# Expert tiles given out unit by unit and run beside the recurrence's chunks, every engine in written order

## The chip, the cores and the metric

The kernel runs on one core of one Trainium2 chip. The metric is the device time of one execution in microseconds (us). Before the change it is 980.18 us, the median of three runs (979.2 to 986.29).

The engines are PE (matrix multiply; PEld is its weight load), DVE (vector), ACT (scalar and activation), POOL (GpSimd) and SP (which here only issues transfers). Sixteen DMA engines move data. ACT and POOL issue transfers too.

## The reference, cut to what matters

```python
# recurrence: batch 4, heads 8, seq 768, head_dim 48, all float32
for t in range(S):
    state = alpha[:, :, t, :, None] * state + k[t] (outer) v[t]
    y[:, :, t] = q[t] @ state
x = y rearranged to (3072, 384)                 # rows = tokens
# router and experts: E = 8, F = 1024
noisy = x @ w_gate + log1p(exp(x @ w_noise)) * noise
top2, top2_w = the two largest of noisy per row, softmax over the two
out[row] = sum over its two experts e of  w * (relu(x[row] @ w1[e]) @ w2[e])
```

## The kernel before, in words

**Recurrence (`fast_gla`).** The 3072 tokens are 24 chunks of 128 (six chunks for each of four sequences). `prepare(n)` turns a, k and q of a chunk with PE transposes into the PSUM tile `tp` (L197). ACT copies a to `a_s` (L203), checks it with a Relu (L205) and copies k (L208). DVE runs the running product P as a scan (L211), multiplies q by it (L214) and takes its reciprocal (L216). POOL multiplies k by the reciprocal (L218). `scores(n)` makes the masked score matrix MT (PE L230, DVE L232) and `k_end` (L236, L238). `finish(n)` makes the state S (PE L247, DVE L253 or L256, POOL L257) and the output y (PE L260 from the old state, L265 from MT). `put_x` copies y out (L155), turns it for the router (L158, L159) and writes it to the DRAM tensor `x_rows` (L160, issued by SP).

**Router.** A unit is three chunks. After each unit, `router` makes the logits (L464), ACT takes exp and log (each with a table load, L468 and L484), DVE finds the top two and their weights, and PE counts ranks (L515, L516), so that every token knows its row in its expert's region of a DRAM `table`. POOL writes the entries with six indirect DMAs for a unit (L527). After the last unit `plan_tiles` computes from the counts which expert and which table row each of 55 tiles of 128 tokens has. `NTILE` = 55 covers the worst case of part-filled tiles.

**Experts.** For each tile, SP loads 128 table entries (L587) and the expert's w1 (L593, 1.5 MB, three buffers, two tiles ahead); POOL gathers the token rows (L596), reads the rows of a first expert from `half_rows` (L635), and writes either to `half_rows` (L641) or the sum to the output (L649). PE turns the rows (L603), does layer 1 (L616, 24 products of 128x128x128) and layer 2 (L623, 8 products with 384 columns); each float32 product shows as two instructions. All of w2 stays in SBUF.

**What sets the order.** A scheduler orders the instructions of each engine inside each of the two parts; the expert part begins after the recurrence part, because the plan needs all counts. `after(n)` puts the clearing of `table` (one transfer of 3200-byte rows, ACT), of `half_rows` (eight transfers of 1536-byte rows, SP) and the router's inputs at step 0, and the loading of w2 (eight transfers of 1.5 MB, SP) at step 2. Transfers issued by SP and ACT share eight semaphores: each new transfer waits until the last one on its semaphore has landed. POOL's transfers have eight others.

Of the kernel before, what the change touches and what calls it, by code (L numbers as in the profile page):

```python
# [18 lines left out]
def kernel(  # L19
# [23 lines left out]

    nc = tc.nc
# [17 lines left out]
    RMAX = N  # L62
    NTILE = (2 * N) // C + E - 1
    TROWS = E * RMAX + (E + 0) * C
    NONE = 2 * N
    RANGE = 1e-18

# [22 lines left out]
    expert_ids = const.tile([C, E], F32, name="expert_ids")  # L90
    region = const.tile([C, E], F32, name="region")
    for e in range(E):
        nc.gpsimd.memset(expert_ids[:, e:e + 1], float(e))
        nc.gpsimd.memset(region[:, e:e + 1], float(e * RMAX))
# [7 lines left out]
    tile_no = const.tile([1, NTILE], F32, name="tile_no")  # L102
    nc.gpsimd.iota(tile_no, pattern=[[1, NTILE]], base=0, channel_multiplier=0, allow_small_or_imprecise_dtypes=True)
    step_no = const.tile([1, RMAX // C], F32, name="step_no")
    nc.gpsimd.iota(step_no, pattern=[[C, RMAX // C]], base=0, channel_multiplier=0,
# [6 lines left out]
    nothing = const.tile([C, TROWS // C * 4], U32, name="nothing")  # L112
    nc.gpsimd.memset(nothing, NONE)
    zeros = const.tile([C, NT // 8, DM], F32, name="zeros")
    nc.gpsimd.memset(zeros, 0.0)

    def clear_table():
        nc.scalar.dma_start(out=table.rearrange("(p r) w -> p (r w)", p=C), in_=nothing)

    def clear_half():  # L120
        for i in range(8):
            nc.sync.dma_start(out=half_rows.rearrange("(i n p) d -> i p n d", i=8, p=C)[i], in_=zeros)

    NIN = 3
# [28 lines left out]
    def put_x(n, y, on, ps_tp, xT, at):  # L153
        y_sb = on.tile([C, DM], F32, name="y_sb")
        nc.scalar.copy(y_sb, y.rearrange("p h d -> p (h d)"))  # L155
        tp = ps_tp.tile([C, NP, C], F32, tag="tp", name="tp")
        for a in range(KO):
            nc.tensor.transpose(tp[:, a, :], y_sb[:, ds(a * C, C)], ident)  # L158
        nc.scalar.copy(xT[:, :, ds(at * C, C)], tp[:, 0:KO, :])  # L159
        nc.sync.dma_start(out=x_rows[ds(n * C, C), :], in_=y_sb)  # L160


    def fast_gla(es, after):
        gc = pool("gc", 1, es)
        vp = pool("vp", 4, es)
        kp = pool("kp", 2, es)
        sp = pool("sp", 2, es)
        xtp = pool("xtp", 2, es)
        rp = pool("rp", 2, es)
        ps_sc = pool("ps_sc", 1, es, space=PS)  # L170
        ps_tp = pool("ps_tp", 3, es, space=PS)
        ps_y = pool("ps_y", 3, es, space=PS)
        ins = {x: [gc.tile([C, H, DP], F32, name=f"{x}_in{i}") for i in range(NIN)] for x in "akq"}
# [4 lines left out]
        a_s = [gc.tile([C, NP, C + 1], F32, name=f"a_s{i}") for i in range(2)]  # L178
        P_s = [gc.tile([C, NP, C + 1], F32, name=f"P_s{i}") for i in range(3)]
        for t in a_s:  # L180
            nc.vector.memset(t[:, :, 0:1], 0.0)
        least = gc.tile([C, NP, C + 1], F32, name="least")
        nc.vector.memset(least, RANGE)
        nc.vector.memset(least[:, :, 0:1], 1.0)
        P_end = gc.tile([C, NT, NP], F32, name="P_end")
        above = gc.tile([C, NT], F32, name="above")
        less_1 = gc.tile([C, 1], F32, name="less_1")
        nc.vector.memset(less_1, -1.0)
        MTs = [gc.tile([C, 2, NP, C], F32, name=f"MT{i}") for i in range(2)]
# [3 lines left out]

        def transposed(src):
            tp = ps_tp.tile([C, NP, C], F32, tag="tp", name="tp")
            for j in range(NP):
                nc.tensor.transpose(tp[:, j, :], src[:, 2 * j:2 * j + 2, :], ident)  # L197
            return tp

        def prepare(n):  # L200
            c = chunks[n]
            a_t = transposed(ins["a"][n % NIN])
            nc.scalar.copy(a_s[n % 2][:, :, 1:C + 1], a_t)  # L203
            over_1 = kp.tile([C, NP, C], F32, name="over_1")
            nc.scalar.activation(over_1, a_t, AF.Relu, bias=less_1, accum_out=above[:, n:n + 1])  # L205
            k_t = transposed(ins["k"][n % NIN])
            k_raw = kp.tile([C, NP, C], F32, name="k_raw")
            nc.scalar.copy(k_raw, k_t)  # L208
            q_t = transposed(ins["q"][n % NIN])
            P = P_s[n % 3]  # L210
            nc.vector.tensor_tensor_scan(P.rearrange("p j t -> p (j t)"), a_s[n % 2].rearrange("p j t -> p (j t)"),  # L211
                                         least.rearrange("p j t -> p (j t)"), 0.0, op0=ALU.mult, op1=ALU.max)
            c["q"] = kp.tile([C, NP, C], F32, name="q_P")
            nc.vector.tensor_mul(c["q"], q_t, P[:, :, 1:C + 1])  # L214
            over = kp.tile([C, NP, C], F32, name="over")
            nc.vector.reciprocal(out=over, in_=P[:, :, 1:C + 1])  # L216
            c["k"] = kp.tile([C, NP, C], F32, name="k_P")
            nc.gpsimd.tensor_tensor(c["k"], k_raw, over, op=ALU.mult)  # L218
            nc.gpsimd.tensor_copy(out=P_end[:, n, :, None], in_=P[:, :, C:C + 1])
            c["end"] = kp.tile([C, NP, 2], F32, name="end")  # L220
# [3 lines left out]
        def scores(n):  # L224
            c = chunks[n]
            sc = [ps_sc.tile([C, NP, C], F32, tag=f"sc{i}", name=f"sc{i}") for i in range(2)]
# [6 lines left out]
            if n % NCH != NCH - 1:  # L233
                tp = ps_tp.tile([C, NP, C], F32, tag="tp", name="tp")
                for j in range(NP):
                    nc.tensor.transpose(tp[:, j, :], c["k"][:, j, :], ident)  # L236
                c["k_end"] = kp.tile([C, NP, C], F32, name="k_end")
                nc.scalar.copy(c["k_end"], tp)  # L238

        def finish(n, xT, at):  # L240
            c = chunks.pop(n)
            first, last = n % NCH == 0, n % NCH == NCH - 1
            y = ps_y.tile([C, H, D], F32, tag="y", name="y")
            if not last:
                s1 = ps_y.tile([C, NP, 2, D], F32, tag="y", name="s1")
                for j in range(NP):
                    nc.tensor.matmul(s1[:, j], c["k_end"][:, j, :], c["v"][:, 2 * j:2 * j + 2, :], start=True,  # L247
                                     stop=True)
                S_new = kp.tile([C, NP * 2, D], F32, name="S_new")
                end = c["end"].rearrange("p j i -> p (j i)")[:, :, None].to_broadcast([C, NP * 2, D])  # L250
                s1 = s1.rearrange("p j i d -> p (j i) d")
                if first:
                    nc.vector.tensor_mul(S_new, s1, end)  # L253
                else:
                    S_sum = kp.tile([C, NP * 2, D], F32, name="S_sum")
                    nc.vector.tensor_add(S_sum, chunks["S"], s1)  # L256
                    nc.gpsimd.tensor_tensor(S_new, S_sum, end, op=ALU.mult)  # L257
            if not first:
                for j in range(NP):
                    nc.tensor.matmul(y[:, 2 * j:2 * j + 2, :], c["q"][:, j, :], chunks["S"][:, 2 * j:2 * j + 2, :],  # L260
                                     start=j == 0, stop=False, skip_group_check=True)
# [5 lines left out]
            if not last:  # L267
                chunks["S"] = S_new
            put_x(n, y, sp, ps_tp, xT, at)

        def load(n):
            chunks[n] = {"v": load_chunk(n, ins, vp)}

        load(0)
        load(1)
        prepare(0)
        load(2)
        prepare(1)
        scores(0)
        for n in range(NT):  # L280
            if n + 3 < NT:
                load(n + 3)
# [439 lines left out]
```

## Time and profile before

| what | value |
|---|---|
| median of the runs | 980.18 us |
| the profiled execution's own time | 982.83 us |
| its span | 981.1 us |
| mean granted PE clock over the span | 0.866 |
| recurrence, router, plan: until the first expert transpose | 0 to 369.6 us |
| 55 tiles: first layer-1 product to the last copy of a tile's sum | 371.2 to 969.2 us |
| after that, last scatter and end | 969.2 to 981.1 us |

The profiled execution took 1.7 us more than its span and 2.65 us more than the median. In the views below each line of a timeline is: start us, duration us, engine, source line, operation, out<-in, shape, count. A line of the windows view is: stretch, length, then busy time of PE, PEld, DVE, ACT, POOL (instruction counts in brackets), the granted PE clock, the DMA engines' busy share, GB/s. A queue line of the DMA view is: queue, packets, MB, share of the time of 16 engines.

### The profile page before, as it was taken

What the parts mean: (1) busy time and instruction counts of PE and PEld (TensorE: products, weight loads), DVE (VectorE), ACT (ScalarE), POOL (GpSimd) and SP (SyncE); (2) the same over time, 40 slices, a digit from 0 to 9 for tenths busy, and PEclk for the clock granted to TensorE, in tenths of its full rate; (3) what the DMA queues carried; (4) which work ended last, traced back from release to release, by engine and by line L of the source; (5) the groups of instructions that cost most, each with busy time, mean ns of one, the idle gap of its engine ahead of it and who ended that gap; (6) DMA issues with size and microseconds to landing.
All of it is one profiled execution on the core that took longest, in us unless ns stands there. A gap on an engine that the chain in (4) does not pass through costs nothing.

```text
span 981.1 us, 14593 instructions
## 1 busy us (share of the span) xinstructions
PE 879.0 (90%) x5393; PEld 738.9 (75%) x5393; DVE 268.1 (27%) x544; ACT 200.4 (20%) x370; POOL 347.9 (35%) x412
## 2 busy tenths in 40 slices
PE   5987879898797609999999999999999999999995
PEld 4876778797697607788788878887887788778873
DVE  7844584755855200011010101010101010101010
ACT  2412241333332201111111111111111111111110
POOL 3213143242342223344334433443444343434322
PEclk9955595676875558999999999999999999999998
DMA  9999162343410027544554555556555655665420
GB/s 236 292 371 211 32 128 56 66 97 63 84 41 9 17 74 264 210 169 157 195 203 156 172 203 192 176 176 217 193 179 185 216 196 180 198 218 168 160 66 3
DMA packets 164463, 152.85 MB, mean 156 GB/s; under 512 B 121704, under 2 KB 137755, under 8 KB 164384
## 3 DMA queue, kind: packets, MB, share of 16 engines
q1 hardware_dynamic: 144736, 127.53, 42.0%
q0 software_dynamic: 15616, 23.76, 7.2%
q10 hardware_dynamic: 4032, 0.53, 0.3%
q8 instruction: 46, 0.75, 0.3%
q14 instruction: 33, 0.27, 0.1%
HBM read 139.83 MB, written 31.57 MB: 175 GB/s over the span
## 4 chain that ended last, share of the span: by engine, by line
issue 44%; PE 22%; POOL 18%; DMA 7%; DVE 4%; ACT 2%; POOLq 1%; ACTq 0%; DVEq 0%; SPq 0%
POOL prev L635 6%; DMA half_rows<-o,tab 5%; POOL x_in L596 5%; PE y L265 5%; PE sc L230 4%; POOL out_dram L649 3%; PE tp L197 3%; PE s L247 3%; PE y L260 2%; PE lg L464 2%; POOL half_rows L641 2%; DVE over L216 1%; PE tp L158 1%; POOL table L527 1%; PE tp L236 1%
## 5 line engine op out<-in xcount | busy, mean ns | idle before, releaser
L616 PEld LDWEIGHTS h_ps<-xt,w 128*128 128x128 f32 x2640 | 304.8, 193 | 15.4 <-DVE xt L605 1.1
L616 PE MATMUL h_ps<-xt,w 128*128 128x128 f32 x2640 | 305.2, 276 | 0.7 <-DVE xt L605 0.7
L623 PE MATMUL o_ps<-w,h 128*128 x880 | 292.9, 486 | 0.0
L623 PEld LDWEIGHTS o_ps<-w,h 128*128 128x128 f32 x880 | 162.9, 190 | 102.0
L641 POOL DMA_INDIRECT half_rows<-o,tab x55 | 66.5, 1210 | 269.6 <-ACT o L634 263.4
L618 ACT ACTIVATE h<-h_ps 128x512 f32<-128x512 f32 x110 | 65.7, 597 | 265.6 <-PE h_ps L616 265.6
L648 DVE TENSOR_TENSOR both<-o,prev 128x384 f32<-128x384 f32 x55 | 30.8, 559 | 294.1 <-ACT o L634 281.3
L605 DVE COPY xt<-x_ps 128x384 f32<-128x384 f32 x55 | 30.7, 559 | 268.9 <-PE x_ps L603 268.9
L634 ACT ACTIVATE o<-o_ps,tab 128x384 f32<-128x384 f32 x55 | 32.0, 581 | 268.8 <-PE o_ps L623 268.8
L527 POOL DMA_INDIRECT table<-entry,place_u x48 | 48.7, 1015 | 104.7 <-DMA table<-entry,place_u 61.8
L216 DVE RECIPROCAL over<-P_s 128x512 f32<-128x512 f32 x24 | 80.4, 3348 | 0.6
L596 POOL DMA_INDIRECT x_in<-x_rows,tab x55 | 56.0, 1018 | 50.9 <-PE x_ps L603 38.3
L230 PE MATMUL sc<-q_P,k_P 48*128 48x128 f32 x384 | 50.7, 379 | 23.7 <-DVE den L486 10.2
L635 POOL DMA_INDIRECT prev<-half_rows,tab x55 | 58.3, 1059 | 38.4 <-DMA half_rows<-o,tab 28.4
L230 PEld LDWEIGHTS sc<-q_P,k_P 48*128 48x128 f32 x384 | 40.6, 260 | 33.3 <-issue 11.5
L265 PE MATMUL y<-vt,MT 128*128 128x48 f32 x384 | 65.5, 340 | 0.0
L265 PEld LDWEIGHTS y<-vt,MT 128*128 128x128 f32 x384 | 64.9, 262 | 0.1
L649 POOL DMA_INDIRECT out_dram<-both,tab x55 | 55.5, 1010 | 18.1 <-issue 16.5
L218 POOL TENSOR_TENSOR k_P<-k_raw,over 128x512 f32<-128x512 f32 x24 | 31.2, 1302 | 61.6 <-DVE over L216 23.5
L603 PE MATMUL x_ps<-ident,x_in 128*128 128x128 f32 x165 | 27.4, 276 | 28.5 <-DMA x_in<-x_rows,tab 28.5
L211 DVE TENSOR_TENSOR_SCAN P_s<-a_s,least 128x516 f32<-128x516 f32 x24 | 32.0, 1334 | 52.8 <-ACT a_s L203 52.7
L603 PEld LDWEIGHTS x_ps<-ident,x_in 128*128 128x128 f32 x165 | 20.1, 143 | 28.6 <-DMA x_in<-x_rows,tab 28.6
(119 smaller groups left out, 627.6 us busy)
## 6 DMA issues: line engine op xcount, KB each, us to landing
w<-in_moe_w_dram SPq DMA_DIRECT2D x63, 1536.0 KB
a_in<-in_alpha_dram SPq DMA_DIRECT2D x24, 192.0 KB
k_in<-in_k_dram SPq DMA_DIRECT2D x24, 192.0 KB
q_in<-in_q_dram SPq DMA_DIRECT2D x24, 192.0 KB
vt<-in_v_dram SPq DMA_DIRECT2D x24, 192.0 KB
half_rows<-zeros SPq DMA_DIRECT2D x8, 576.0 KB
x_rows<-y_sb SPq DMA_DIRECT2D x24, 192.0 KB
tab<-table SPq DMA_DIRECT2D x55, 2.0 KB
```

Of the source, the lines that this page charges most:

```text
L216: nc.vector.reciprocal(out=over, in_=P[:, :, 1:C + 1])
L230: nc.tensor.matmul(sc[i][:, j, :], c["k"][r, j, :], c["q"][r, j, :], start=True, stop=True)
L265: nc.tensor.matmul(y[:, h, :], MTs[n % 2][:, i, j, :], c["v"][:, h, :], start=first and h == 0, stop=h == H - 1, skip_group_check=True)
L527: nc.gpsimd.indirect_dma_start(out=table, out_offset=bass.IndirectOffsetOnAxis(ap=place_u[:, i:i + 1], axis=0), in_=entry.bitcast(U32)[:, ...
L596: nc.gpsimd.indirect_dma_start(out=x_in[i % NB], out_offset=None, in_=x_rows, in_offset=bass.IndirectOffsetOnAxis(ap=tabs[i][:, 0:1], axis=0),
L603: nc.tensor.transpose(x_ps[:, a, :], x_in[i % NB][:, ds(a * C, C)], ident)
L616: nc.tensor.matmul(h_ps[:, fo, :], w1[:, a, ds((half * FO // 2 + fo) * C, C)], xt[:, a, :], start=a == 0, stop=a == KO - 1)
L618: nc.scalar.activation(h[:, ds(half * FO // 2, FO // 2), :], h_ps, AF.Relu)
L623: nc.tensor.matmul(o_ps, h[:, fo, :], w2[:, ds(e, 1), fo, :].rearrange("p o d -> p (o d)"), start=fo == 0, stop=fo == FO - 1)
L635: get = nc.gpsimd.indirect_dma_start(out=prev[i % 2], out_offset=None, in_=half_rows, in_offset=bass.IndirectOffsetOnAxis(ap=tab[:, 3:4], ...
L641: put = nc.gpsimd.indirect_dma_start(out=half_rows, out_offset=bass.IndirectOffsetOnAxis(ap=tab[:, 2:3], axis=0), in_=o, in_offset=None, b ...
L649: put = nc.gpsimd.indirect_dma_start(out=out, out_offset=bass.IndirectOffsetOnAxis(ap=tab[:, 3:4], axis=0), in_=both, in_offset=None, boun ...
```

## The change

1. **Tiles per unit.** `plan_tiles(u)` now runs after every unit, on all 128 partitions. It gives out as many tiles as must already be full: `GIVEN` = 0, 5, 11, 17, 23, 29, 35, and all 55 after the last unit. Only the last unit's plan holds part-filled tiles. A table entry now holds token, weight, the other expert and the rank there; whether a token's first half has been stored is worked out per tile from these (`gather_x`: five small DVE instructions).
2. **Interleaving.** One list of steps n. Step n holds `prepare(n+2)`, `state(n)`, `turn_y(n-1)`, `scores(n+1)`, `route(n-1)`, `output(n)`, `load(n+3)`, `give(n-1)`, and beside them, in turn, the four quarters of each tile of that step. Steps 0 to 7 have no tile, step 10 has one, the other steps from 8 to 25 have two each (35 in all), and the last step holds the other 20.
3. **Order.** `tc.manual_schedule()` keeps every engine's instructions as written.
4. **Buffers.** PSUM (eight banks): `tp` 3 to 2, the bank tag `y` (s1, y, logits, ranks, totals) 3 to 1, layer-2 sums 2 to 1. SBUF: chunk inputs 3 to 2, w1 3 to 2, P 3 to 1, `a_s` and others 2 to 1, `x_in` 4 to 3. The Relu check writes back to the PSUM tile that it reads.
5. **Clearing.** `table` is cleared from a 16-byte pattern repeated 25,600 times, `half_rows` from a 512-byte pattern repeated 9,216 times, both issued by ACT after `prepare(1)`. `x_rows` writes move from SP to ACT. w2 is loaded at step 1, before `load(4)`.
6. **Waits.** The scatters into the table no longer wait for one another, but for the clearing.

```diff
+    GIVEN = [max(0, (2 * UT * (u + 1) - E * (C - 1) + C - 1) // C) for u in range(NU - 1)] + [NTILE]
...
     def clear_table():
-        nc.scalar.dma_start(out=table.rearrange("(p r) w -> p (r w)", p=C), in_=nothing)
+        entries.clear()
+        cleared = nc.scalar.dma_start(out=table.bitcast(F32).rearrange("(p r) w -> p r w", p=C),
+                                      in_=nothing[:, None, :].to_broadcast([C, TROWS // C, 4]))
+        entries.append(cleared.ins)
+    def put_entries(place, entry):
...
+        for earlier in entries[1:] + taken:
+            tc.declare_no_dep(put.ins, earlier, reason="different rows of the table")
+        tc.add_manual_dep(put.ins, entries[0].name, AFTER, reason="the table is cleared first")
...
     def clear_half():
-        for i in range(8):
-            nc.sync.dma_start(out=half_rows.rearrange("(i n p) d -> i p n d", i=8, p=C)[i], in_=zeros)
-    NIN = 3
+        nc.scalar.dma_start(out=half_rows.rearrange("(p n) (a d) -> p (n a) d", p=C, d=C),
+                            in_=zeros[:, None, :].to_broadcast([C, NT * KO, C]))
+    NIN = 2
...
+    def tile_steps(i, do, units):
+        def first():
+            load_w1(i + 1)
+            if i + 2 < units[1]:
+                gather_x(i + 2, units[0])
+            layer1(i, 0)
+        def second():
+            layer1(i, 1)
+        def third():
+            if i + 1 < units[1]:
+                turn_x(i + 1)
+            get_half(i)
+            layer2(i, 0)
+        def fourth():
+            layer2(i, 1)
+            combine(i)
+    def pools(es, name):
+        on = {"one": pool(name + "one", 1, es), "two": pool(name + "two", 2, es), "three": pool(name + "three", 3, es),
+              "tab": pool(name + "tab", 6, es)}
+        for x, bufs in (("h", 2), ("o", 1), ("tp", 2), ("sc", 1), ("y", 1)):
+            on[x] = pool(name + "ps_" + x, bufs, es, space=PS)
...
+        with tc.manual_schedule():
+            load(0)
+            load(1)
+            prepare(0)
+            load(2)
+            prepare(1)
+            load_router()
+            clear_table()
+            clear_half()
+            scores(0)
+            for n, tiles in enumerate(beside):
+                work = [step for i in tiles for step in steps_of(i)]
+                chunk = [lambda: prepare(n + 2), lambda: state(n), lambda: turn_y(n - 1), lambda: scores(n + 1),
+                         lambda: route(n - 1), lambda: output(n), lambda: load(n + 3), lambda: give(n - 1)]
+                if n == 1:
+                    load_w2()
...
+                if nxt and nxt[0] in starts:
+                    lo, u = nxt[0], unit_of[nxt[0]]
+                    some = range(lo, min(lo + 4, GIVEN[u]))
+                    chunk.insert(1, lambda: [load_tab(i) for i in some])
+                    chunk.insert(4, lambda: (load_w1(lo), [gather_x(i, u + 1) for i in some[:2]]))
+                    chunk.append(lambda: turn_x(lo))
+                for j in range(max(len(work), len(chunk))):
+                    if j < len(work):
+                        work[j]()
+                    if j < len(chunk):
+                        chunk[j]()
```

Arithmetic is the same in both. `state` is the first half of the old `finish`, `output` the second, `turn_y` and the logits part of `route` are taken from `put_x` and `router` and now run for each chunk, `choose` and `enter` are the rest of `router`, and `give` is `enter` and `plan_tiles`.

## The prediction, blind

> **What bounds the kernel now.** I read the page's shares first, then its 40 slices, then windows by stage, then the timeline of each stage.
>
> ```profile
> PE 879.0 (90%) x5393; PEld 738.9 (75%) x5393; DVE 268.1 (27%) x544; ACT 200.4 (20%) x370; POOL 347.9 (35%) x412
> ...
> PEclk9955595676875558999999999999999999999998
> DMA  9999162343410027544554555556555655665420
> ```
>
> PE bounds the whole, at two speeds: until slice 15 the granted clock is mostly about half, after it full. The windows show where the time stands.
>
> ```profile
> 44.00:76.00 32.00, 26.10 (x127) 23.01 (x128) 15.41 (x44) 7.08 (x14) 7.89 (x10) 0.54 1.07 372
> 148.00:172.00 24.00, 23.08 (x110) 21.98 (x111) 9.92 (x20) 4.26 (x10) 8.49 (x11) 0.50 0.27 58
> 339.00:369.00 30.00, 1.77 (x8) 1.59 (x8) 5.19 (x23) 0.00 (x0) 8.74 (x9) 0.50 0.22 75
> 369.00:969.00 600.00, 598.71 (x3685) 481.59 (x3685) 60.94 (x109) 97.08 (x164) 231.60 (x216) 1.00 0.53 181
> ```
>
> Four things: early on the DMA engines are full (372 GB/s); chunks then run with PE nearly busy at clock 0.50; for 30 us before the tiles PE idles for ranks, plan and gathers; and the tiles are 600 us of PE without a gap. The timeline gives a tile and a chunk at full clock:
>
> ```profile
> 947.67 5.52 PE L616 MATMUL h_ps<-xt,w 128*128 128x128 f32 x48
> 953.03 0.49 PE L603 MATMUL x_ps<-ident,x_in 128*128 128x128 f32 x3
> 953.36 5.33 PE L623 MATMUL o_ps<-w,h 128*128 x16
> 958.52 5.52 PE L616 MATMUL h_ps<-xt,w 128*128 128x128 f32 x48
> ```
>
> ```profile
> 28.42 0.49 PE L158 MATMUL tp<-ident,y_sb 128*128 128x128 f32 x3
> 28.74 0.60 PE L197 MATMUL tp<-ident,a_in 128*128 128x128 f32 x4
> ...
> 34.64 1.10 PE L247 MATMUL s<-vt,k_end 128*128 128x96 f32 x8
> 35.58 0.49 PE L158 MATMUL tp<-ident,y_sb 128*128 128x128 f32 x3
> ```
>
> A tile is 958.52 - 947.67 = 10.85 us. A chunk is 35.58 - 28.42 = 7.16 us, plus 0.8 for its logits (L464, six passes): 7.95.
>
> **The change, in four stretches of time.**
>
> *Stretch A: to the end of step 7, no tile beside.* It has two terms.
>
> First, transfers. In the new order of SP, w2 stands before load(4), and in the order of semaphores its third transfer waits for the table's clearing and its fifth for the clearing of half_rows. So load(4), which step 2 needs first, comes behind all early traffic, and PE stands still after steps 0 and 1. I add that traffic at full engines. The first four chunk loads and noise end near 19 us, as they do now. w2: 8 x 1.57 MB at 372 GB/s, 33.8. The clearing of half_rows, 576 pieces of 512 bytes per engine: a 192-byte piece costs 15 ns (the loads ran at about 208 GB/s over 16 engines) and a 1536-byte one 66 ns (372 GB/s); on the line between them 27 ns, 15 us. The table, 1600 pieces of 16 bytes per engine, is not in the trace; its nearest rows are the 32-byte reads at the start (window 0 to 3 us) and the 64-byte packets of the table's scatters (343 to 360 us):
>
> ```profile
> q10 hardware_dynamic: 319, 0.01, 6.0%
> ```
>
> ```profile
> q0 software_dynamic: 192, 0.01, 1.2%
> ```
>
> 6.0% of 16 x 3 us over 319 packets is 9 ns; 1.2% of 16 x 17 us over 192 is 17 ns. So 14 to 27 us by these, up to 106 us if a piece cost what a 1536-byte one does. I take 10 ns, 16 us, as the 32-byte reads are nearest in size and use the same kind of queue. x_rows 1, two hand-overs 2, arrival of a(4) 2. Sum 19 + 34 + 15 + 16 + 1 + 2 + 2 = 89 us.
>
> In the Trainium skill, the page DMA: Bandwidth & Descriptors, section Specifications, says that a transfer under 512 bytes does not reach line rate because the engine then reads, modifies and writes. That speaks against the 16-byte pattern; no row here shows such a write from SP or ACT, and the sum by a doubled price would be 16 us more.
>
> Second, six steps (2 to 7). With one bank `y`, the logits wait for S_sum, and DVE has S_sum behind the reciprocal. From the step's first transpose, at half clock: a turned 1.1, copied 0.6 (L203), Relu 0.7 (L205), only then the q transposes at 2.5 because `tp` has two buffers; they end at 3.6; q_P 0.7 (L214), reciprocal 3.35 (L216), S_sum 0.55 (L256): 8.3. PE meanwhile does s1, turn_y, scores and k_end to 8.8; logits to 10.2, their copy to 10.65, y 1.7 + 3.5 (L260, L265 at half clock): 15.8 us. At full clock the same chain gives 11.7. The windows from 46 to 330 us have a mean clock of about 0.65, so three tenths full: 14.6. Six: 87.6, less 1.7 as chunk 6 has no old state: 86. Routing adds the rank, a DVE wait and the total: 3.5 at step 3; at step 6 also the plan, 24 small DVE instructions at 0.15 to 0.34 ahead of the next scan: 7. The first w1 comes behind plan and table reads: 3.5. A = 89 + 86 + 10.5 + 3.5 = 189 us.
>
> The page TensorE: Matmul & The Clock Gate, Part 1, says the clock rises after about 3.4 us of sustained work. The row 148 to 172 us contradicts it: 23.08 of 24 us busy at 0.50. By the rule the six steps would be 17 us shorter.
>
> *Stretch B: steps 8 to 25.* 35 tiles x 10.85 = 380. Chunk work beside them at full clock, as layer products keep PE dense like 369 to 969 us. In 14 full steps: 7.95, plus one wait for the q transposes, since ACT must finish Relu h0 (0.6), copy a (0.6) and the in-place Relu (0.7) while PE has 0.9 of transposes: 1.2; plus about 12 changes between tile and chunk work at some 0.15 (idle "issue" gaps of 0.17 to 0.33 stand before such groups): 1.8. 14 x 10.95 = 153. Chunks that end or start a sequence lack parts: -5. Steps 22 to 24: 13. Six `give`: PE does ranks, then waits for ACT's o (0.58), DVE's sum (0.56) and product (0.2) before the total: 2.4 each, 14. Six first tiles of a unit: turn_x stands just before layer 1, so the copy (L605, 0.56) and two hand-overs show: 6. Late w1 at steps 10 and 25: 4. B = 566 us (380 + 153 - 5 + 13 + 14 + 6 + 4 = 565, rounded up).
>
> *Stretch C:* 20 tiles x 10.85 = 217. w1 with two buffers is issued when layer 1 of the tile before last is done, a whole tile ahead; its 1.57 MB take 4.3 us at 372 GB/s, so it is covered. *D:* the end, 12 as now (969.2 to 981.1).
>
> **What costs nothing, and why.** On POOL the table scatters lose 61.8 us of waiting for one another (waits view, L527), but POOL is busy 35% and not the bound; what is queued behind them, the k product, is needed half a step later. Where they wait for the clearing instead (unit 0, step 3), it is over by then. The six scatters a unit at 1.0 us delay SP's table reads to about 11 us into the next step and its w1 issue to 16; the tile starts at 31. SP loses 24 x_rows issues and eight clearings. ACT gains the x_rows issues (0.44 each), 24 logits copies (0.2) and the clearings' issues; ACT is busy 20%. If issuing 1600 pieces per engine blocks ACT, steps 0 and 1 shift under the wait for load(4). DVE's five small instructions per tile are 0.75 us in 10.85. w1 of each unit's first tile is loaded twice, 6 x 1.57 MB, while DMA is about half busy. Bounds of these together: 0 to +10 us; no gain is possible, as no engine but PE sets the pace in B and C.
>
> **Sum.** 189 + 566 + 217 + 12 = 984 us of span against 981.1; with 1.7 around it 986 against 982.83. This execution stands 2.65 above the median, so 983 us against 980.18: no change. The gain in B (chunks at full clock, the 30 us hole gone) is spent in A, where eight chunks take 189 us; now the eighth chunk's output is copied near 130.
>
> **Rivals.**
> - *The table's clearing is slow (slower).* Place: the 16-byte pieces ahead of w2's third transfer. For: smallest pieces anywhere. Against: 9 and 17 ns above. At 66 ns each it adds 90: 1073 us. From 14 ns on (7 us more) the change is slower by 1%.
> - *The fixed order costs PE more beside tiles (slower).* If each step of B has 2 us more waiting than walked through: 16 x 2 = 32, 1015 us. For: single buffers of `y`, P, xt, o_ps. Against: my walk finds each free by several us.
> - *A is cheaper (faster).* Full clock in steps 2 to 7 (-17) and no cost at the changes in B (-25): 941; half of it 962. For: PE ran at full clock from 0 to 46 us. Against: the half clock of 148 to 172.
> - *The tiles are not there to give out:* 2 x 384 (u+1) entries less 8 x 127 are always in full tiles, so no: below 0.01.
>
> **How the numbers follow.** Forecast 983, by itself 958 to 1005: 0.50 (faster 0.14, same 0.22, slower 0.14). Slow clearing 0.08, order costs 0.17 (both slower; 0.25). Cheaper 0.25 (faster 0.24, within 1% 0.01). By sign, with 1% (about what a measurement of this kernel can tell from no change): faster 0.38, same 0.23, slower 0.39. For 8 in 10 I leave out most of the slow clearing and the outermost part of the other rivals: 940 to 1035.
>
> **What would show it.** Step by step in the profile after: step 2's first transposes near 89 us, with PE idle from about 40; table's clearing landed 16 us after its turn; steps 2 to 7 at 12 to 16 us each and first layer-1 product at 189; two-tile steps at 32.6 us with one gap of 1.2 before the q transposes; tiles of 10.85 at the end from 755. Wrong would be: load(4) early, gaps of over 2 us elsewhere in B, a clock below 1 there, or tiles at the end slower than 10.85.

## The result, and the profile after

The changed kernel takes 1040.28 us (median of 4 runs, 1037.48 to 1045.17) against 979.69 us before (4 runs, 976.91 to 986.29): a ratio of 1.061 (95% interval 1.054 to 1.069). The forecast was 983 us with a range to 1035: the change is slower, and the time lies just outside the range. The profiled execution took 1037.48 us, its span is 1035.7 us.

The page of the kernel after, with the lines that answer to those of before (busy shares, then 40 slices of 25.9 us):

```profile
PE 833.8 (81%) x5405; PEld 693.4 (67%) x5405; DVE 320.1 (31%) x973; ACT 201.4 (19%) x394; POOL 343.4 (33%) x444
...
PE   3004049875998799999999899998997899999995
...
PEclk8555555676999899999999999999999899999998
DMA  9999993326543844665395638426544545656530
GB/s 121 6 5 44 372 299 72 77 54 183 169 124 98 270 159 131 199 202 167 98 304 156 188 117 257 161 100 208 178 166 136 217 157 169 213 174 210 176 126 4
```

The DMA row and the GB/s row have to be read together. In slices 1 and 2 (counted from 0) the engines are full, and they move 6 and 5 GB/s. PE does next to nothing in the same slices. From slice 10 on PE is nearly full at full clock, with 35 of the 55 tiles beside the chunks, as the change says.

The windows by stretch, in the columns of the windows view (PE, PEld, DVE, ACT, POOL, clock, DMA share, GB/s):

```profile
14.00:91.00 77.00, 2.65 (x17) 2.12 (x14) 5.51 (x5) 0.56 (x2) 1.56 (x3) 0.52 1.87 13
91.00:155.00 64.00, 21.92 (x126) 19.70 (x127) 13.69 (x12) 6.31 (x15) 3.92 (x7) 0.55 1.05 287
155.00:251.00 96.00, 74.20 (x432) 67.32 (x431) 55.11 (x134) 26.40 (x57) 29.29 (x47) 0.62 0.35 83
251.00:805.00 554.00, 510.07 (x3464) 423.59 (x3464) 204.35 (x671) 127.82 (x253) 220.44 (x260) 0.97 0.54 173
805.00:1024.00 219.00, 218.20 (x1337) 175.48 (x1337) 30.57 (x140) 35.21 (x60) 79.07 (x75) 0.99 0.48 166
```

Set against the terms of the prediction:

| stretch | predicted us | measured us |
|---|---|---|
| A, until load(4) lets step 2 start | 89 | 154.8 |
| A, steps 2 to 7 until the first layer-1 product | 100 (86 + 10.5 + 3.5) | 96.1 (154.78 to 250.92) |
| B, steps 8 to 25 | 566 | 554.6 (to 805.49) |
| C, 20 tiles | 217 | 218.2 (to 1023.69) |
| D, end | 12 | 12.0 |

One term is off by 66 us, the others together by 14 the other way. What happened in it, from ACT's timeline (ACTq is ACT's own queue: the time in which it was issuing a transfer):

```profile
11.87 2.02 ACTq L134 DMA_DIRECT2D table<-nothing  x1
14.23 76.17 ACTq L153 DMA_DIRECT2D half_rows<-zeros  x1
90.44 0.59 ACT L277 COPY k_end<-tp 128x512 f32<-128x512 f32 x1 [80.20 <-issue]
...
101.59 29.47 ACTq L188 DMA_DIRECT2D x_rows<-y_sb  x1
```

The clearing of the table is issued at 11.87. ACT then stands 76.17 us in the issue of the next transfer, the clearing of half_rows. Behind that issue in ACT's written order stands the copy of k_end, and behind the copy stands PE. In step 1 ACT is held a second time, 29.47 us in the issue of x_rows, while the clearing of half_rows and w2 fill the engines. The timeline of PE, transposes for chunks 2, 3 and 4 and then the first tile:

```profile
15.69 0.95 PE L234 MATMUL tp<-ident,a_in 128*128 128x128 f32 x4
91.08 1.12 PE L234 MATMUL tp<-ident,k_in 128*128 128x128 f32 x4 [74.44 <-ACT k_end L277]
...
100.85 1.08 PE L234 MATMUL tp<-ident,a_in 128*128 128x128 f32 x4
101.72 1.06 PE L234 MATMUL tp<-ident,k_in 128*128 128x128 f32 x4
132.48 1.11 PE L234 MATMUL tp<-ident,q_in 128*128 128x128 f32 x4 [29.70 <-ACT tp L243]
...
154.78 1.09 PE L234 MATMUL tp<-ident,a_in 128*128 128x128 f32 x4 [10.34 <-DMA a_in<-in_alpha_dram]
...
250.92 5.02 PE L696 MATMUL h_ps<-xt,w 128*128 128x128 f32 x24 [6.06 <-DMA w<-in_moe_w_dram]
```

In the bracket: how long the engine was idle before it, and what it waited for. Steps 0 and 1, predicted to run by 40 us, straddle the clearing. Only then are w2's transfers issued (SP, 101.50 to 141.31), then load(4) (141.35). What SP waits for from 0 to 200 us (what waits, for what: us in total, times, longest):

```profile
SPq L167 <- PE y L310: 108.1, 3, 86.2
SPq L182 <- DMA half_rows<-zeros: 17.2, 1, 17.2
```

SP's load of v for chunk 3, which stands ahead of w2, waits 86.2 us for the output of step 0. The fifth transfer of w2 waits 17.2 us for the clearing of half_rows.

How dear one piece is, from the DMA view of 30 to 80 us, where nothing but the clearing moves:

```profile
DMA packets 16020, 0.26 MB, mean 5 GB/s; under 512 B 16020, under 2 KB 16020, under 8 KB 16020
...
q10 hardware_dynamic: 16020, 0.26, 195.4%
```

16 engines x 50 us / 16,020 = 49.9 ns for each 16-byte piece; 1600 pieces per engine are 80 us. The share of 195.4% is the packets' own time: 97.6 ns each, with about two in flight on an engine at once.

### The profile page after: what moved, and what is told of

Its sections match the earlier page's. It is cut to its first block, busy times and chain, and to the rows that moved or that the text cites. A ratio compares the mean times of both kernels' runs of the same rounds, so it can differ in the third digit from the quotient of the medians.

```text
span 1035.7 us, 15003 instructions
## 1 busy us (share of the span) xinstructions
PE 833.8 (81%) x5405; PEld 693.4 (67%) x5405; DVE 320.1 (31%) x973; ACT 201.4 (19%) x394; POOL 343.4 (33%) x444
## 4 chain that ended last, share of the span: by engine, by line
PE 63%; DMA 9%; ACTq 7%; issue 6%; DVE 4%; ACT 4%; SPq 3%; POOL 2%; another core or an unknown queue 2%; POOLq 0%; DVEq 0%
PE h_ps L696 26%; PE o_ps L708 23%; ACTq L153 7%; DMA w<-in_moe_w_dram 4%; PE y L310 3%; SPq L182 2%; PE tp L234 2%; DMA prev<-half_rows,where 2%; PE sc L269 2%; PE x_ps L685 2%; PE y L305 1%; ACT tp L243 1%; DMA a_in<-in_alpha_dram 1%; PE lg L202 1%
## 5 line engine op out<-in xcount | busy, mean ns | idle before, releaser
L696 PEld LDWEIGHTS h_ps<-xt,w 128*128 128x128 f32 x2640 | 312.6, 197 | 25.5 <-issue 14.4
L726 POOL DMA_INDIRECT half_rows<-o,where x55 | 63.3, 1152 | 285.2 <-ACT o L725 285.2
L732 DVE TENSOR_TENSOR prev<-prev,o 128x384 f32<-128x384 f32 x55 | 30.8, 561 | 300.3 <-ACT o L725 153.2
L255 POOL TENSOR_TENSOR k_P<-k_P,over 128x512 f32<-128x512 f32 x24 | 30.4, 1265 | 256.1 <-DVE over L254 178.7
L248 DVE TENSOR_TENSOR_SCAN P<-a_s,least 128x516 f32<-128x516 f32 x24 | 29.6, 1233 | 181.7 <-issue 140.2
L254 DVE RECIPROCAL over<-P 128x512 f32<-128x512 f32 x24 | 80.2, 3343 | 0.0
L234 PE MATMUL tp<-ident,k_in 128*128 128x128 f32 x96 | 18.6, 329 | 74.4 <-ACT k_end L277 74.4
L676 POOL DMA_INDIRECT x_in<-x_rows,where x55 | 57.4, 1043 | 45.0 <-issue 23.5
L234 PEld LDWEIGHTS tp<-ident,k_in 128*128 128x128 f32 x96 | 14.4, 172 | 75.1 <-ACT k_end L277 74.7
L733 POOL DMA_INDIRECT out_dram<-prev,where x55 | 55.1, 1003 | 28.4 <-DVE prev L732 9.6
L715 POOL DMA_INDIRECT prev<-half_rows,where x55 | 56.9, 1034 | 22.5 <-issue 19.8
L234 PE MATMUL tp<-ident,q_in 128*128 128x128 f32 x96 | 19.4, 335 | 48.5 <-ACT tp L243 47.9
L139 POOL DMA_INDIRECT table<-entry,place_u x48 | 48.3, 1006 | 14.5 <-issue 12.2
```

The source lines that it names most:

```text
L139: put = nc.gpsimd.indirect_dma_start(out=table, out_offset=bass.IndirectOffsetOnAxis(ap=place, axis=0), in_=entry, in_offset=None, bounds_ ...
L676: nc.gpsimd.indirect_dma_start(out=x_in[i % NB], out_offset=None, in_=x_rows[0:units * UT, :], in_offset=bass.IndirectOffsetOnAxis(ap=wher ...
L696: nc.tensor.matmul(h_ps[:, fo, :], w1[:, a, ds((part * FO // 2 + fo) * C, C)], xt[:, a, :], start=a == 0, stop=a == KO - 1)
L715: get = nc.gpsimd.indirect_dma_start(out=prev[i % 2], out_offset=None, in_=half_rows, in_offset=bass.IndirectOffsetOnAxis(ap=wheres[i][:, ...
L726: put = nc.gpsimd.indirect_dma_start(out=half_rows, out_offset=bass.IndirectOffsetOnAxis(ap=where[:, 1:2], axis=0), in_=o, in_offset=None, ...
L733: put = nc.gpsimd.indirect_dma_start(out=out, out_offset=bass.IndirectOffsetOnAxis(ap=where[:, 2:3], axis=0), in_=prev[i % 2], in_offset=N ...
```

## The experiments

Theory: the 16-byte pieces cost 50 ns each, and what was forecast of everything else holds. Rivals: the half_rows clearing or w2's place do it; the fixed order with its single buffers does it; the pieces hurt only because ACT's work stands behind them.

**Table in pieces of 640 bytes** (e1_table640)

```diff
-    nothing = const.tile([C, 4], F32, name="nothing")
+    nothing = const.tile([C, 40, 4], F32, name="nothing")
...
-        out=table.bitcast(F32).rearrange("(p r) w -> p r w", p=C),
-        in_=nothing[:, None, :].to_broadcast([C, TROWS // C, 4])
+        out=table.bitcast(F32).rearrange("(p r s) w -> p r (s w)", p=C, s=40),
+        in_=nothing.rearrange("p s w -> p (s w)")[:, None, :].to_broadcast([C, TROWS // C // 40, 160])
```

> The changed kernel with one thing put back in part: the table is cleared by 640 pieces of 640 bytes instead of 25,600 pieces of 16. Theory (a 16-byte piece costs an engine about 48 ns, 1600 of them per engine 77 us, and all later transfers stand behind them): the clearing lasts about 2 us, step 2 starts about 75 us earlier (near 80 instead of 154.8), everything after it is unchanged, 1040 - 75 = 965 us. Rival 1 (the 9,216 pieces of the half_rows clearing fill ACT's queue and hold the chunks nearly as long): step 2 starts near 115, 1000 us. Rival 2 (single buffers and the fixed order cost the time, the clearing only overlaps with it): over 1030 us.

Measured 968.62 us (965.65 to 973.05), ratio to before 0.988 (0.983 to 0.994). The theory's 965 holds and both rivals fall. ACT's issue of half_rows takes 0.53 us instead of 76.17:

```profile
14.76 1.93 ACTq L134 DMA_DIRECT2D table<-nothing  x1
18.62 0.53 ACTq L153 DMA_DIRECT2D half_rows<-zeros  x1
```

Step 2 starts at 74.10 (the prediction's 89 less the 16 for the table is 73), the first layer-1 product at 172.72. The size of one transfer's pieces turns 6% slower into 1% faster. The rest of the change takes in sum what the prediction said: its 983 less the 16 for the table is 967.

**Pieces of 64 bytes** (e2_table64: the same edit with 4 table rows to a piece)

> The changed kernel with the table cleared by 6,400 pieces of 64 bytes. If the price is per piece and the same at 64 bytes as at 16 (48 ns): 400 pieces per engine, 19 us instead of 77, total near 982 us. If the price goes by bytes (400 KB at about 5 GB/s): still 77 us, 1040 us. If only a piece under some size is dear and 64 bytes cost what the scatters' 64-byte packets cost (17 ns): 7 us, near 970 us.

Measured 974.94 us. Neither a constant 48 ns (982) nor a price by bytes (1040); near the third case, 5 us above it. From 20 to 23 us 3,619 of these pieces pass, beside 1,199 packets of the chunk loads: at most 16 x 3 / 3,619 = 13.3 ns each.

**16-byte pieces that lie apart** (e3_strided)

```diff
-    table.rearrange("(p r) w -> p r w", p=C)
+    table.rearrange("(r p) w -> p r w", p=C)
```

> The changed kernel with the same 25,600 pieces of 16 bytes, but consecutive pieces of a partition lie 2048 bytes apart in the table instead of 16. If a write of 16 bytes has its price wherever it goes: clearing 77 us, 1040 us. Rival (neighbouring writes into the same few bytes of memory wait for one another): a piece costs 9 to 17 ns, the clearing 15 to 27 us, total 980 to 990 us.

Measured 1004.84 us: between the two. The same 25,600 pieces in another order are 35 us faster, so nearly half of their price is that a 16-byte piece follows directly on its neighbour. The rest stays. From 30 to 50 us:

```profile
DMA packets 11511, 0.18 MB, mean 9 GB/s; under 512 B 11511, under 2 KB 11511, under 8 KB 11511
```

16 x 20 / 11,511 = 27.8 ns a piece.

**The kernel before, with 16-byte pieces** (e4_before16)

```diff
-    nc.scalar.dma_start(out=table.rearrange("(p r) w -> p (r w)", p=C), in_=nothing)
+    nc.scalar.dma_start(out=table.rearrange("(p r) w -> p r w", p=C),
+                        in_=nothing[:, None, 0:4].to_broadcast([C, TROWS // C, 4]))
```

> The kernel before with one thing of the change alone: its table is cleared by 25,600 pieces of 16 bytes instead of 128 rows of 3200. If the pieces occupy the engines wherever they stand: chunk loads and w2 come 60 to 77 us later, 1040 to 1057 us. Rival (they hurt only because in the new order ACT's own work stands behind their issue and w2 before load(4)): the old schedule hides most of it, 980 to 1000 us.

Measured 1077.75 us (ratio 1.098, 1.091 to 1.105): above even the upper case. The pieces need no fixed order to hurt. Here no other transfer waits behind them on ACT, but PE waits for the chunk loads themselves, as the waits view of 0 to 140 us shows (engine, what waits, for what: us in total, times, longest; the last line is from the same view of SP):

```profile
PE tp L198 <- DMA a_in<-in_alpha_dram: 38.4, 3, 23.6
PE tp L198 <- DMA k_in<-in_k_dram: 25.2, 2, 18.1
PE tp L198 <- DMA q_in<-in_q_dram: 18.5, 4, 9.6
...
SPq L136 <- DMA table<-nothing: 60.1, 1, 60.1
```

PE's three lines are 82 us. The loads, on another queue, share the same 16 engines: from 40 to 50 us the engines pass 1,036 packets of theirs and 2,362 of the clearing's. And a load of SP that has nothing to do with the table waits 60.1 us for its clearing, until 116.89; the next load of a is issued at 127.84, and the longest of PE's waits, 23.6 us, ends with it at 133.77. So in this kernel the pieces hurt in two ways: they slow the loads that share the engines, and they hold the next loads back through a wait on the clearing.

**w2 spread over the steps** (e5_w2_spread, on e1)

```diff
-                if n == 1:
-                    load_w2()
+                if 1 <= n <= 6:
+                    chunk.insert(7, lambda: load_w2([n - 1] if n < 5 else [2 * n - 6, 2 * n - 5]))
```

> The table in 640-byte pieces (968.6 us), and w2 no longer in one run of eight transfers ahead of load(4): one transfer follows each of load(4) to load(7), two each follow load(8) and load(9). In that kernel PE waits 28.6 us for load(4) at step 2. Theory (w2 in front of load(4) is the second of the two transfer terms): that wait goes, 940 us. Rival (the chunk loads then share the engines with the clearing of half_rows and with w2, and later steps wait instead): 955 to 968 us.

Measured 946.15 us, 22.5 less than e1 where 28.6 were expected. Step 2 starts at 49.42 instead of 74.10, 24.7 earlier; steps 2 to 7 then take 103.8 instead of 98.6 us. The theory holds with a fifth of the wait given back.

**No tile beside a chunk** (e6_none_beside, on e1)

```diff
-    GIVEN = [max(0, (2 * UT * (u + 1) - E * (C - 1) + C - 1) // C) for u in range(NU - 1)] + [NTILE]
+    GIVEN = [0] * (NU - 1) + [NTILE]
...
-        while not beside[-1]:
+        while len(beside) > NT + 2:
```

> The table in 640-byte pieces, and no tile given out before the last unit: GIVEN is 0 seven times, then 55, so all tiles run after the chunks, still in written order. Theory (beside tiles a chunk costs PE its 11 us at full clock; alone it takes about 15 at half clock, and the wait for the last plan comes back): 165 us to the end of step 7, 17 steps of 15.3 us, about 20 us for plan and first gathers, 55 tiles of 10.85, end 12: near 1054 us against 968.6. Rival (written order loses beside the tiles what the clock gains): 960 to 1000 us.

Measured 1049.85 us: 81 more than e1. So the interleaving itself is worth 81 us. The new order without it costs: chunks alone run at half clock and take 15.6 us each (transposes of a from 166.62 to 369.49, 13 chunks), against 12.2 under the scheduler before (122.12 to 293.33, 14 chunks). How much of that is the written order and how much the fewer buffers was not tried. The windows of this kernel:

```profile
165.00:432.00 267.00, 222.33 (x1116) 204.59 (x1115) 130.66 (x276) 69.52 (x149) 71.05 (x119) 0.52 0.29 53
432.00:1040.00 608.00, 600.11 (x3687) 483.11 (x3687) 91.95 (x445) 97.00 (x164) 232.41 (x218) 0.99 0.53 182
```

**The Relu check from SBUF** (e7_relu, on e1)

```diff
-            nc.scalar.activation(a_t, a_t, AF.Relu, bias=less_1, accum_out=above[:, n:n + 1])
+            over = one.tile([C, NP, C], F32, name="over")
+            nc.scalar.activation(over, a_s[:, :, 1:C + 1], AF.Relu, bias=less_1, accum_out=above[:, n:n + 1])
...
-            over = one.tile([C, NP, C], F32, name="over")
```

> The table in 640-byte pieces, and the Relu check reads the SBUF copy a_s and writes to the buffer of the reciprocal, so that the PSUM buffer of a is free after the copy. PE's wait of its q transposes for that Relu is 13.5 us in 14 steps beside tiles and 3.7 us before. Theory (this is a wait on PE's path, as every PE wait beside tiles is): -16 us, 953 us. Rival (the next wait of the step, for the logits or the scores, takes its place): 963 to 968 us.

Measured 953.00 us (952.54 to 957.09): 15.6 less than e1, as expected. The waits that it was aimed at, first in e1 from 173 to 727 us (first layer-1 product to the start of the last step), then what stands there in e7 from 167 to 722 us:

```profile
PE tp L234 <- ACT tp L243: 13.5, 14, 1.0
```

```profile
PE tp L234 <- ACT a_s L242: 3.7, 13, 0.3
```

The number came as forecast, but the traces do not show that it came from these waits. The two profiled executions are 8.6 us apart (spans 963.9 and 955.3), and the stretch beside the tiles takes the same in both:

```profile
172.70:726.90 554.20, 508.56 (x3459) 422.62 (x3459) 202.99 (x662) 127.79 (x253) 218.91 (x259) 0.98 0.58 170
167.10:721.90 554.80, 515.29 (x3460) 428.29 (x3460) 203.05 (x662) 130.40 (x253) 218.21 (x258) 0.96 0.59 174
```

Nearly 10 us less of this wait are taken up there by 6.7 us more of PE's busy time, at a lower clock, and by waits of 3.8 us for ACT's h that e1 does not have. 5.6 of the 8.6 us come ahead of the first product, the rest in the last step. Of the other executions, which are 15 to 21 us apart, there is no trace.

**Three mended together** (e8_all: both clearings from wide rows, taken from the part of w2's buffer that is loaded last; w2 spread; the Relu check from SBUF)

```diff
-            clear_table()
-            clear_half()
+            clear_table(w2[:, E - 2, 0:3])
+            clear_half(w2[:, E - 1, 0:2])
...
```

> The changed kernel with three things mended together: both clearings take wide rows (table 3200 bytes, half_rows 3072) from the part of w2's buffer that is loaded last, w2 spread over steps 1 to 6, and the Relu check from SBUF. If the gains add (1040 - 71 - 29 - 16): 922 us. Rival (the freed stretch is taken by the half clock and by loads that come one behind another): 935 to 950 us.

Measured 927.00 us (ratio to before 0.946, 0.940 to 0.953): 922 was expected, so the gains add to within 5 us; by the gains as measured (71.7, 22.5 and 15.6) the sum is 930.5.

**16-byte pieces 64 bytes apart** (e9_line_apart)

```diff
+        for i in range(4):
-    table.rearrange("(p r) w -> p r w", p=C)
+    table.rearrange("(p r i) w -> i p r w", p=C, i=4)[i]
...
```

> The changed kernel with its 25,600 pieces of 16 bytes in another order: four transfers, the first of every fourth table row from row 0, the next from row 1 and so on, so that consecutive pieces of a partition lie 64 bytes apart instead of 16. If pieces into the same 64 bytes that follow one another directly are what costs 48 ns: a piece falls to about 17 ns, what a 64-byte piece cost, the clearing to 27 us, total near 990 us. If a 16-byte piece costs at least the 25 ns that it cost at a distance of 2048 bytes: 40 us, about 1005 us. If 64 bytes are still too near: 48 ns, 1040 us.

Measured 998.15 us; from 25 to 50 us 14,580 pieces, at most 27.4 ns each. The second case: 64 bytes apart is as good as 2048, and a 16-byte piece still costs over 25 ns.

**Pieces of 32 bytes** (e10_table32: the edit of e1 with 2 table rows to a piece)

> The changed kernel with its table cleared by 12,800 pieces of 32 bytes, in the original order, consecutive ones adjoining. If the price is per piece for all pieces under 64 bytes (48 ns): 800 per engine, 38 us, 1002 us. If a piece costs 17 ns as one of 64 bytes does unless its neighbour lies in the same 64 bytes, two of these share one: between 17 and 48 ns, 14 to 38 us, 977 to 1002 us; that size alone matters would show as the upper end, a wait per neighbour as about 33 ns, 26 us, 990 us.

Measured 967.45 us: below every case named. From 20 to 24 us, table pieces alone:

```profile
DMA packets 5461, 0.17 MB, mean 44 GB/s; under 512 B 5461, under 2 KB 5461, under 8 KB 5461
...
q10 hardware_dynamic: 5461, 0.17, 189.6%
```

16 x 4 / 5461 = 11.7 ns for 32 bytes, though two neighbours share 64 (22.2 ns of packet time each). My reading from e2 and e3, that neighbours in the same 64 bytes are the trouble, falls. The step lies between 32 and 16 bytes. A piece is both read from SBUF and written to DRAM, and in all these kernels the 16-byte pieces of a partition are read from the same 16 bytes each time; so the order of the writes is shown to matter, but whether the remaining price of 27 ns lies with the read or the write is not.

**Without the stale load** (e11_no_stale_w1, on e8)

```diff
         def first():
-            load_w1(i + 1)
+            if i + 1 < units[1]:
+                load_w1(i + 1)
```

> The mended kernel (927.0 us) without the useless load: the last tile of a unit no longer loads w1 for the next unit's first tile from a plan that is not yet made, so the right load can take the free buffer as soon as the plan is there. In the mended kernel PE waits 14.2 us for w1 beside and after the chunks, in four places. Theory (the stale load holds the buffer): these waits shrink to under 5 us, 917 us. Rival (the load comes late because the plan does, and the buffer is free by then): 925 to 928 us.

Measured 909.36 us (904.42 to 911.54; ratio to before 0.926, 0.921 to 0.931), 17.6 less than e8 and somewhat more than the wait that it was to remove; the two profiled executions differ by 13.5 us in span. In e8 from 140 to 930 us that wait is

```profile
PE h_ps L708 <- DMA w<-in_moe_w_dram: 14.2, 4, 6.1
```

and from 120 us on the kernel without the stale load has no such line at all. From the first layer-1 product to the start of the last step e8 takes 549.7 us and e11 533.1 (143.82 to 676.91), so the gain lies where the wait was. This is the fastest median of the study.

**State before prepare, in all steps** (e12_state_first, on e11)

```diff
-  chunk = [lambda: prepare(n + 2), lambda: state(n), ...
+  chunk = [lambda: state(n), lambda: prepare(n + 2), ...
```

> The same as the kernel without the stale load, and each step does state(n) before prepare(n+2), so that DVE's S_sum is no longer behind the scan and the reciprocal and the one bank of the logits comes free earlier. In the mended kernel the logits wait 9.6 us for S_sum in steps 2 to 7. Theory: that wait goes and PE waits some 0.7 us per step for the copy of y instead: 5 us faster than without. Rival (the scan starts later, so the k product and the scores wait, in every step): 5 to 20 us slower than without.

Measured 911.66 us (910.38 to 919.52): no faster than without. Neither case fits, and the trace shows why the total hides two effects. First the windows of e11, then those of e12, cut at the first layer-1 product and at the last step's start:

```profile
0.00:144.00 144.00, 104.07 (x605) 93.59 (x606) 84.50 (x161) 39.22 (x81) 42.55 (x110) 0.66 0.72 206
144.00:677.00 533.00, 505.90 (x3460) 419.78 (x3460) 203.18 (x662) 130.23 (x253) 218.89 (x259) 0.99 0.52 164
```

```profile
0.00:127.00 127.00, 81.09 (x605) 70.47 (x606) 86.24 (x160) 39.21 (x81) 43.85 (x110) 0.86 0.83 234
127.00:677.00 550.00, 514.51 (x3462) 423.97 (x3463) 207.75 (x664) 130.54 (x253) 221.19 (x259) 0.98 0.51 159
```

The stretch to the first product is 17 us shorter at a clock of 0.86 instead of 0.66. All four executions have a higher mean clock over the span than those of e11 (0.945 to 0.960 against 0.930 to 0.942). Beside the tiles the new order takes 17 us longer. PE is busy 8.6 us more there, 514.51 against 505.90 at a clock of 0.98 instead of 0.99, and ten waits of turn_x for ACT's copy of k are 7.2 us.

**State before prepare, steps 0 to 6 only** (e13_state_first_early on e11, e14_early_on_640 on e1)

```diff
+                if n < 7:
+                    chunk[0], chunk[1] = chunk[1], chunk[0]
```

> The kernel without the stale load (909.4 us), with state(n) before prepare(n+2) in steps 0 to 6 only. Theory (the waits for S_sum hold the clock down; beside tiles the old order is the better one): first layer-1 product near 127 us instead of 143.8, the rest as without: 893 us. Rival (the order beside tiles was not what gave the 17 us back; what comes early waits later for the plan, for w1 or for the tokens): 905 to 912 us.

> The changed kernel with the table in 640-byte pieces (968.6 us) and state(n) before prepare(n+2) in steps 0 to 6. There w2 still stands before load(4), and the Relu check still holds a PSUM buffer of the transposes. Theory (full clock when the logits no longer wait for S_sum): steps 2 to 7 take about 80 us instead of 98.6, total 951 us. Rival (the q transposes' wait for the Relu, 0.6 to 1.4 us in each step, holds the clock down as well): total 963 to 969 us.

Measured 912.95 us (906.53 to 915.26) and 964.69 us (960.23 to 973.58): no gain that these runs can tell, as both rivals had it (the first time lies just above its 905 to 912). In the profiled execution of e13 the first layer-1 product does come 14.5 us earlier (129.30 against 143.82), and step by step the lead shrinks: 14.4 us at 282 us, 11.6 at 531, 5.7 at the start of the last step, where PE waits 3.98 us for ACT's h that e11 does not wait for. That execution is the fastest of its four, at a clock of 0.958; the other three have 0.938 to 0.942, much as e11 has, so the early lead may not stand in all of them. In e14 the lead is 8.0 us at the first product (164.68 against 172.72) and nothing at the end. So the half clock of steps 2 to 7, which the prediction's rival "A is cheaper" wanted gone, was lifted in part by order alone in these executions, but an earlier start is not an earlier end. Why the lead runs out is shown only in part.

## Why the prediction was wrong

**The step that failed: "I take 10 ns, 16 us, as the 32-byte reads are nearest in size and use the same kind of queue."** A 16-byte piece cost 49.9 ns, not 10: 1600 x 39.9 ns = 64 us too little, and 983 + 64 = 1047 against 1040 measured. The mechanism stood among the rivals, with its place and its formula ("From 14 ns on (7 us more) the change is slower by 1%"), at a chance of 0.08. The row that it rests on is of 32-byte reads; the clearing differs from it in size and in direction, and neither alone is dear in these runs. 32-byte pieces were written at 11.7 ns each (e10). And the trace before holds 16-byte reads, which the prediction passed over: each table read (L587) fetches 128 entries of 16 bytes. From 361 to 362.2 us the first of them is alone on the engines:

```profile
q1 hardware_dynamic: 144, 0.00, 6.1%
```

6.1% of 16 x 1.2 us over 144 packets is 8.1 ns, in a short burst of 9 packets per engine. What was dear is a long run of 16-byte pieces that are written, and no row of that trace prices it: the scatters' 64-byte packets hold four table rows of 16 bytes each (6 scatters x 128 rows x 16 bytes = 192 x 64) and come from POOL's queue. The bound of 66 ns was the honest end, and it deserved more than 8 in 100.

**What the queue did.** "If issuing 1600 pieces per engine blocks ACT, steps 0 and 1 shift under the wait for load(4)": ACT was blocked, in the issue behind it, for 76.17 us. This did not vanish under another wait, because w2, which was to fill that time, is itself issued only after step 0's output (SP: 101.50). The account by semaphores was half right. The third transfer of w2 waits for no clearing, as the table's is over before w2 is issued; the fifth waits 17.2 us for the clearing of half_rows, as predicted, and load(4) stands behind it. ACT's second hold, 29.47 us in the issue of x_rows, does shift part of step 1 under that wait: of all the time up to 154.78, PE waits only 10.34 us for load(4) itself. The terms still add up one behind the other: 89 with 80 in place of 16 is 153, and step 2 started at 154.8. That it fits so closely is partly luck: the table's clearing began while the first chunk loads still ran, and from 95 to 100 us the clearing of half_rows moved 63 GB/s where it was priced near 300.

**w2 before load(4): right.** The wait is 28.6 us in e1, and 22.5 us were gained when it was taken away.

**Steps 2 to 7: right in sum** (96.1 against 100), at half clock as argued:

```profile
155.00:170.00 15.00, 14.14 (x72) 13.08 (x72) 6.89 (x6) 2.98 (x7) 2.35 (x4) 0.50 0.32 63
```

PE is busy 14.14 of 15 us at 0.50. By the rule of the Trainium skill (TensorE: Matmul & The Clock Gate, Part 1) some 3.4 us of sustained work should have raised it; it did not, as before the change. Where e12 took the waits for S_sum away, the clock rose. (Two small slips change nothing: the mean clock from 46 to 330 us is 0.63, not 0.65, and w1's 1.57 MB at 372 GB/s take 4.2 us, not 4.3.)

**Stretch B, C, D: right, B 11 us too dear.** The waits for the q transposes were put at 1.2 us in 14 steps and measure 13.6 us in 14 (251 to 790 us):

```profile
PE tp L234 <- ACT tp L243: 13.6, 14, 1.0
PE total L582 <- DVE picked L551: 10.1, 6, 4.6
PE h_ps L696 <- DMA w<-in_moe_w_dram: 9.1, 2, 6.1
```

Whether taking them away shortens this stretch is open: e7's median says so, its trace does not. The rival that the fixed order costs more beside tiles did not occur.

**"What costs nothing": one item wrong.** The doubled w1 loads were let pass because DMA is half busy. Their price is not bandwidth but the buffer that the stale load holds: 17.6 us in the mended kernel (e11), against a bound of 10 for all such items together. In the changed kernel itself this price is inside the 554.6 us of B, and its waits for w1 there are 9.1 us.

**The other page.** The Trainium skill (DMA: Bandwidth & Descriptors, Specifications) says that transfers under 512 bytes miss line rate because the engine then reads, modifies and writes. That they miss it agrees: 32-byte pieces moved 44 GB/s (e10), 512-byte pieces of half_rows about 342 (e1: 4011 packets in 6 us, 23.9 ns each). But the dear step here is not at 512 bytes: per piece 32 and 64 bytes cost less than 512, and 16 bytes cost most. Collectives: The Full Stack, Rules for kernel authors, says that 32-byte alignment of buffers prevents a read-modify-write. It speaks of a collective's buffers and not of the size of a piece; a step below 32 bytes, which is what was measured, would fit it, but no run here shows what the engine or the memory does in it.

## What to carry to other kernels

Price a transfer by its pieces, and do not carry the price of one piece size to a smaller one, nor of a read to a write: here 16-byte reads and 32-byte writes were both cheap, and 16-byte writes were not. Where the trace has no row of that size and direction, give the far bound its full weight. A long transfer of small pieces is not background work: it took the engines from the other queue's loads, it held back transfers that had to wait for its end, and in a fixed order the instruction behind the next issue waited with it. When a change as large as this moves the time little, or the wrong way, look for the one small term that cancels it; here it was the piece size of a clearing, and the rest of the change was worth keeping.

## What the runs showed of the hardware

- Pieces written from SBUF to DRAM by ACT's queue cost, per engine: 16 bytes one after the other 49.9 ns (the kernel after), 16 bytes apart 27.4 to 27.8 ns (e9, e3), 32 bytes 11.7 ns (e10), 64 bytes at most 13.3 ns (e2), 512 bytes 23.9 ns (e1). Why 16 bytes that lie apart still cost more than twice 32 bytes was not tried. A 16-byte read of the table by SP took 8.1 ns (before, 361 to 362.2 us).
- The issue of a transfer can hold its engine for most of the time that the queue ahead of it takes: 76.17 us behind the 16-byte pieces, 40.06 behind the strided ones (e3), 8.91 behind 12,800 pieces of 32 bytes (e10), 5.58 behind 6,400 of 64 (e2), 0.53 behind those of 640 bytes (e1).
- A transfer can wait for an earlier one on another engine's queue that it shares no data with: a load of v on SP waited 60.1 us for the table's clearing on ACT (e4).
- PE can be busy 14.14 of 15 us and stay at a clock of 0.50 (after, 155 to 170 us; 23.08 of 24 us before).
- A higher mean PE clock is not a shorter run: of the changed kernel's four runs, the one at 0.937 took 1045.17 us, the one at 0.88 took 1037.48.
